# Attention and two MoE layers on one core: the passage to MoE 2 rearranged

## The chip, the cores and the metric

The kernel runs on one core of one Trainium2 chip. Its time is the device time of one execution in microseconds (us); 933.41 us is the median of three runs before the change (931.83 to 934.14). The engines are TensorE (PE; PEld loads its weights), VectorE (DVE), ScalarE (ACT), GpSimd (POOL) and SyncE (SP), each with its own queue of instructions, worked off in order. Transfers are issued from SP, POOL or ACT and run on 16 DMA engines.

## The reference

Three layers follow one another on 2176 tokens of width 512 (4 batches of 32 global and 512 local tokens):

1. Attention: local tokens see the global ones and a window of 32 on either side; global tokens see all.
2. MoE 1: `x = leaky_relu(x @ w_in, 0.01) @ w_out`, with 2048 inner columns.
3. MoE 2, over 8 experts of 512 x 1024 and 1024 x 512. Each token goes to one expert:

```
logits = normalised(x) @ normalised(expert_emb).T / tau
idx    = argmax(logits);  gate = softmax(logits)[idx]
out    = gate * (relu(x @ w1[idx]) @ w2[idx])
```

Inputs and outputs are float32. Products that need it are computed from a high and a low part in the fp32r format, three matmuls for one.

## The kernel before, in words

**Stages.** Attention and MoE 1 run fused, in pairs of token tiles of 128 (17 tiles; the last pair step has three, tiles 14 to 16). A step (i, f) of MoE 1 is `L1` (one slice of 128 inner columns, its leaky ReLU on ScalarE and VectorE) and, a step later, `L2` (its product with `w_out`). Finished tiles are routed: R0 to R3 normalise a tile, transpose it, take its logits, and count its tokens' ranks within their expert; an indirect transfer writes token numbers into a list sorted by expert (`idl`), and the tile's rows go to DRAM (`x2d`).

MoE 2 works on blocks of 128 tokens of one expert, taken from that list. There are up to 24 blocks, in two lanes (even and odd), each lane with its own copy of one expert's weights (`w1a`, `w2a`; `w1b`, `w2b`), loaded by `load_w(s)` only where the plan says that the lane's expert changes. `make_plan(True)` plans the first 6 blocks from tiles 0 to 13 during the last steps of MoE 1; `make_plan(False)`, the late plan, plans the other 18 when the last three tiles are routed.

**The last three tiles.** `Q0` copies a tile from PSUM into x2 and sums its squares; `Q1` transposes it and takes its logits into `lp`; `Q2` finds the expert of all three tiles' tokens, ending with an exponential on ScalarE; `Q3` takes ranks (`rp`) and counts (`cp`) on TensorE; `Q4` turns ranks into list places, issues three indirect scatters into `idl` on POOL and six stores into `x2d` on SP.

**A block.** `block(s)` holds, in this order: `M1(s, 0)` (first half of x @ w1, 12 matmuls, then the ReLU into `hs`); `M2(s-1, 0)`; the split of the next block's first half of w1 (`split_w1`, each split two casts on ScalarE and two subtractions on VectorE, L849 and L850); `HT(s, 0)` (four transposes of hs, evicted to `ht`); `X2(s+1)` (four transposes of the next block's tokens, evicted to `xgT`); `M1(s, 1)`; `M2(s-1, 1)`, which ends in `yo`, scaled on ScalarE and scattered to the output by POOL; `split_w2(s+1, 0)`; `HT(s, 1)`; the two other splits; `load_w(s+3)`. In block 0 `M1(0, 1)` comes ahead. Block s reads its tokens by `gather(s)`, an indirect transfer on POOL from `x2d` by the ids that `load_ids(s)` fetched on SP. At the points "a" to "f" of a block the table `due` puts in routing steps.

**What sets the order.** TensorE is in program order throughout, SP in all blocks, VectorE in blocks 0 to 3 (`manual_schedule`). The other queues are ordered by a scheduler from priorities and estimated readiness; `keep_in_program_order` pins one instruction behind the one traced before it on its engine.

**Buffers.** Tiles with one tag share `bufs` buffers. "half" has 8: the eight halves of MoE 1's weights, then lane b's weights and the split weights of blocks (six buffers). "xs" has 2 and holds `xgT` and tile 16's x2; "x2" has 2 and holds the x2 of tiles 14 and 15 and then `yo`; "x2T" has 2. In PSUM the tags "T", "S", "H" and "Y" have two banks each.

Of the kernel before, what the change touches and what calls it, by code (L numbers as in the profile page):

```python
# [8 lines left out]
F32 = mybir.dt.float32  # L9
# [9 lines left out]
P = 128  # L19
# [5 lines left out]
def kernel(  # L25
# [20 lines left out]
    NT, DM = out.shape  # L46
    DFF = w_in.shape[1]
    E, _, F2 = w1.shape
    HP = H // 2
    NC = SL // P  # L50
    KM = DM // P
    KF = DFF // P
    KF2 = F2 // P
# [360 lines left out]
    rt = {}  # L414
# [121 lines left out]
    NL = 3  # L536
# [19 lines left out]
    def Q1(q):  # L556
        x2 = rt[q, "x2"]
        xp = ps.tile([P, KM, P], F32, tag="T", name="x2p")
        for k in range(KM):
            nc.tensor.transpose(xp[:, k, :], x2[:, k * P:(k + 1) * P], ident)  # L560
        xT = sb.tile([P, KM, P], F32, tag="x2T", bufs=2, name="x2T")
        nc.vector.tensor_copy(xT, xp)
        if q == 0:
            rt["lp"] = ps.tile([P, NL, E], F32, tag="S", name="lp")
        for k in range(KM):
            nc.tensor.matmul(rt["lp"][:, q, :], xT[:, k, :], enT[:, k, :], start=(k == 0), stop=(k == KM - 1))

# [25 lines left out]
    def Q3():  # L593

        ob = lt_["ob3"]
        rp = ps.tile([P, NL, E], F32, tag="T", name="rp")
        nc.tensor.matmul(rp, tri, ob[:, 0:NL], start=True, stop=False)
        nc.tensor.matmul(rp, ones, ob[:, NL].unsqueeze(1).to_broadcast([P, NL, E]), start=False, stop=False)
        for q in range(1, NL):
            nc.tensor.matmul(rp[:, q, :], ones, ob[:, 0, :], start=False, stop=(q == 1 and NL == 2))  # L600
        for q in range(2, NL):
            for o in range(1, q):
                nc.tensor.matmul(rp[:, q, :], ones, ob[:, o, :], start=False, stop=(q == NL - 1 and o == q - 1))
        cp = ps.tile([1, E], F32, tag="T", name="cp")
        for q in range(NL + 1):
            nc.tensor.matmul(cp, ones[:, 0:1], ob[:, q, :], start=(q == 0), stop=(q == NL))
        rt["rp"], rt["cp"] = rp, cp

    def Q4():
        V = nc.vector  # L610
# [115 lines left out]
    def make_plan(early):  # L726
# [21 lines left out]
        if early:  # L748
            mx, ky, k2 = work(1), work(E), work(E)
            V.tensor_reduce(out=mx, in_=nb, axis=AX.X, op=ALU.max)  # L750
            V.scalar_tensor_tensor(out=ky, in0=nb, scalar=mx, in1=rf, op0=ALU.is_equal, op1=ALU.mult)
            V.tensor_reduce(out=mx, in_=ky, axis=AX.X, op=ALU.max)
            V.tensor_scalar(out=ky, in0=ef, scalar1=mx, scalar2=None, op0=ALU.add)
            V.tensor_scalar(out=k2, in0=ky, scalar1=float(E), scalar2=-float(E), op0=ALU.is_ge, op1=ALU.mult)
            V.tensor_tensor(out=ky, in0=ky, in1=k2, op=ALU.add)
            V.tensor_tensor(
                out=lt, in0=ky.unsqueeze(1).to_broadcast([1, E, E]), in1=ky.unsqueeze(2).to_broadcast([1, E, E]),
                op=ALU.is_lt,
            )
        else:  # L760
            V.tensor_tensor(out=nb, in0=nb, in1=taken, op=ALU.subtract)
        V.tensor_tensor(out=pre, in0=lt, in1=nb.unsqueeze(1).to_broadcast([1, E, E]), op=ALU.mult)
        V.tensor_reduce(out=st8, in_=pre, axis=AX.X, op=ALU.add)
        V.tensor_tensor(out=en8, in0=st8, in1=nb, op=ALU.add)
        if early:
            posf = ihf[:, 0:n]
        else:
            pos = work(NLANE, NH)
            tot, h12, hf = work(1), work(NH), work(1)
            V.tensor_reduce(out=tot, in_=nb, axis=AX.X, op=ALU.add)  # L770
            V.tensor_scalar(out=h12, in0=ihf, scalar1=2.0, scalar2=tot, op0=ALU.mult, op1=ALU.is_lt)
            V.tensor_reduce(out=hf, in_=h12, axis=AX.X, op=ALU.add)
            V.tensor_scalar(out=pos[:, 0], in0=ihf, scalar1=hf, scalar2=1000.0, op0=ALU.is_ge, op1=ALU.mult)
            V.tensor_tensor(out=pos[:, 0], in0=pos[:, 0], in1=ihf, op=ALU.add)
            V.tensor_scalar(out=pos[:, 1], in0=ihf, scalar1=hf, scalar2=None, op0=ALU.add)
            V.tensor_copy(plan[:, 0, NBLK:NBLK + 1], tot)
            posf = pos.rearrange("o l i -> o (l i)")
        shp = [1, n, E]
        a1, a2 = work(n, E), work(n, E)
        pb = posf.unsqueeze(2).to_broadcast(shp)  # L780
# [4 lines left out]
        V.tensor_reduce(out=vd, in_=a1, axis=AX.X, op=ALU.add)  # L785
        V.tensor_tensor(out=a2, in0=a1, in1=ef.unsqueeze(1).to_broadcast(shp), op=ALU.mult)
        V.tensor_reduce(out=ex, in_=a2, axis=AX.X, op=ALU.add)
        if early:
            lanewise, at = "o (i l) -> o l i", 0
            V.tensor_reduce(out=taken, in_=a1.rearrange("o n e -> o e n"), axis=AX.X, op=ALU.add)  # L790
            V.tensor_copy(oe, st8)
        else:
            lanewise, at = "o (l i) -> o l i", NE
            V.tensor_tensor(out=oe, in0=st8, in1=taken, op=ALU.subtract)
# [10 lines left out]
        def got(v):  # L805
            return v.rearrange(lanewise, l=NLANE)

        m = n // NLANE
        V.tensor_copy(el[:, :, at + 1:at + 1 + m], got(ex))
        V.tensor_tensor(out=got(ch), in0=got(ex), in1=el[:, :, at:at + m], op=ALU.not_equal)  # L810
# [15 lines left out]
    def load_w(s):  # L826
        if s >= NBLK:
            return
        w1r, w2r = lanes[lane(s)]
        e = nc.sync.value_load(plan[0:1, 1, s:s + 1], min_val=0, max_val=E - 1)  # L830
        cond = nc.sync.value_load(plan[0:1, 2, s:s + 1], min_val=0, max_val=1)
        nc.sync.dma_start(w1r, w1[bass.ds(e, 1)].rearrange("o (k p) f -> p (o k) f", p=P), cond=cond)
        nc.sync.dma_start(w2r, w2[bass.ds(e, 1)].rearrange("o (k p) f -> p (o k) f", p=P), cond=cond)
# [33 lines left out]
    def split_w1(s, j):
        for piece in pieces_w1(s, j):
            piece()

    def split_w2(s, j):
        for piece in pieces_w2(s, j):
            piece()

    def X2(s):
        if s >= NBLK:
# [12 lines left out]
    def M1(s, j):  # L889
        xT = xts[s][0]  # L890
        w = w1s.pop((s, j))
        hp_ = ps.tile([P, DM], F32, tag="H", name="hp2")
        for a, c in ((0, 0), (1, 0), (0, 1)):
            for k in range(KM):
                nc.tensor.matmul(  # L895
                    hp_, xT[:, a, k, :], w[:, c, k, :], start=(a + c + k == 0), stop=(c == 1 and k == KM - 1)
                )
        hs = sb.tile([P, DM], F32, tag="g", bufs=2, name="hs")
        if j == 0:
            nc.scalar.activation(out=hs, in_=hp_, func=AF.Relu)  # L900
        else:
            nc.vector.tensor_scalar(out=hs, in0=hp_, scalar1=0.0, scalar2=None, op0=ALU.max)
        hss[s, j] = hs
# [143 lines left out]
    while k < len(steps):  # L1047
        i, f = steps[k]
        if k == KF * (2 * B - 1) + 6:
            assert not pend_r  # L1050
            plan_constants()
            make_plan(True)
            load_w(0)
            for s in range(NEARLY):
                load_ids(s)
            for s in range(4):
                gather(s)
# [28 lines left out]
            st(t)  # L1086
        if k >= KF * (2 * B - 1) + 10:
            if k == KF * (2 * B - 1) + 10:
                first = pieces_w1(0, 0) + pieces_w1(0, 1) + pieces_w2(0, 0) + pieces_w2(0, 1)
            for piece in first[:2 if len(first) > 6 else 1]:  # L1090
                tc.keep_in_program_order(piece())
            first = first[2 if len(first) > 6 else 1:]
        if slot == LAST and not hold and att is not None:
            att_pool.__exit__(None, None, None)
            att = None
# [4 lines left out]
            )  # L1100
            lanes[0] = lane_a
        k += 1
    lanes[1] = (
        sb.tile([P, KM, F2], F32, tag="half", bufs=8, name="w1b"),
        sb.tile([P, KF2, DM], F32, tag="half", bufs=8, name="w2b"),
    )
    for piece in first:
        piece()
    load_w(1)
    load_w(2)  # L1110
    X2(0)
    L2(*state["prev"])
    for t in range(NL):
        with tc.high_priority(offset=0):
            Q0(t, ys.pop((2 * B - 1, t)))

    def late_plan():
        make_plan(False)
        for q in range(NEARLY, NEARLY + 3):
            load_ids(q)  # L1120

    def block(s, end, begin=0):

# [36 lines left out]
        load_w(s + 3)  # L1160

    due = {
        (0, "a"): [(Q1, (0,)), (Q1, (1,))], (0, "b"): [(Q1, (2,))], (0, "c"): [(Q2, ())],
        (0, "d"): [(Q3, ())], (0, "e"): [(Q4, ())], (1, "a"): [(late_plan, ())],
    }
    NMAN = 4
    NCUT = NBLK - NLANE
# [43 lines left out]
```

## Time and profile before

| | |
|---|---|
| profiled execution | 931.04 us, its span 929.1 us, mean granted clock 0.963 |
| PE busy | 863.6 us, 93% |
| PEld busy | 727.1 us, 78% |
| DVE busy | 639.2 us, 69% |
| ACT busy | 561.6 us, 60% |
| POOL busy | 173.5 us, 19% |
| chain that ended last | PE 73%, DVE 9%, issue 6%, DMA 6%, ACT 5% |

The page cuts the span into 40 slices of 23.2 us and gives the busy share of each in tenths:

```
PE   3766799999999999999999999997899999999997
DVE  6998888444664654554544435556989989999996
PEclk9776799999999999999999999997999999999999
```

Attention alone fills the first five slices, attention with MoE 1 and MoE 1 alone go up to about 621 us, MoE 2 takes the rest. A granted clock of 1.0 is TensorE at 2.4 GHz, 0.5 at 1.2 GHz. In a timeline, equal instructions that follow one another are merged to one row (x12), and the idle time in brackets is that of the engine just ahead of the row, with what ended it. A row of the table by stretches gives the window, its length, the busy us of PE, PEld, DVE, ACT and POOL with their instruction counts, the mean granted clock, the DMA engines' busy share and GB/s.

### The profile page before, as it was taken

What the parts mean: (1) busy time and instruction counts of PE and PEld (TensorE: products, weight loads), DVE (VectorE), ACT (ScalarE), POOL (GpSimd) and SP (SyncE); (2) the same over time, 40 slices, a digit from 0 to 9 for tenths busy, and PEclk for the clock granted to TensorE, in tenths of its full rate; (3) what the DMA queues carried; (4) which work ended last, traced back from release to release, by engine and by line L of the source; (5) the groups of instructions that cost most, each with busy time, mean ns of one, the idle gap of its engine ahead of it and who ended that gap; (6) DMA issues with size and microseconds to landing.
All of it is one profiled execution on the core that took longest, in us unless ns stands there. A gap on an engine that the chain in (4) does not pass through costs nothing.

```text
span 929.1 us, 15882 instructions
## 1 busy us (share of the span) xinstructions
PE 863.6 (93%) x5578; PEld 727.1 (78%) x5578; DVE 639.2 (69%) x1557; ACT 561.6 (60%) x1206; POOL 173.5 (19%) x220
## 2 busy tenths in 40 slices
PE   3766799999999999999999999997899999999997
PEld 2555587888888888888888988986687888888885
DVE  6998888444664654554544435556989989999996
ACT  5877876544544644445433232364687888888885
POOL 3423433000210110010000000120233222231311
PEclk9776799999999999999999999997999999999999
DMA  8875562120122121110000000554315118829550
GB/s 215 197 215 149 146 189 69 33 45 17 29 61 44 25 57 29 44 30 3 13 12 1 24 1 24 193 187 73 24 58 215 35 46 328 276 78 384 191 202 26
DMA packets 104995, 92.68 MB, mean 100 GB/s; under 512 B 73735, under 2 KB 82055, under 8 KB 104914
## 3 DMA queue, kind: packets, MB, share of 16 engines
q1 hardware_dynamic: 97618, 77.47, 27.7%
q0 software_dynamic: 4224, 10.78, 4.2%
q10 hardware_dynamic: 3072, 3.41, 1.2%
q8 instruction: 45, 0.74, 0.4%
q14 instruction: 36, 0.29, 0.1%
HBM read 140.03 MB, written 11.63 MB: 163 GB/s over the span
## 4 chain that ended last, share of the span: by engine, by line
PE 73%; DVE 9%; issue 6%; DMA 6%; ACT 5%; POOL 1%; SPq 1%; POOLq 0%; ACTq 0%; DVEq 0%
PE hps L669 20%; PE hp L895 10%; PE yp L923 9%; PE yp L691 7%; PE yp L693 6%; PE yp L692 6%; PE av L247 3%; PE pp L233 2%; PE sp L199 2%; PE tp L909 2%; DMA qn<-in_q_l_dram 1%; DMA ids<-idl 1%; ACT pr L217 1%; PE lp L499 1%; DVE pr L223 1%
## 5 line engine op out<-in xcount | busy, mean ns | idle before, releaser
L676 ACT COPY gf<-hps 128x256 f32<-128x256 f32 (+1 forms) x144 | 50.2, 360 | 175.2 <-PE hps L669 168.4
L677 DVE SCALAR_TENSOR_TENSOR gf<-gf 128x256 f32<-128x256 f32 (+1 forms) x144 | 60.7, 429 | 129.3 <-ACT gf L676 127.7
L895 PE MATMUL hp<-w1s,xgT 128*128 128x512 f32 x528 | 139.1, 413 | 0.0
L923 PE MATMUL yp<-w2s,ht 128*128 128x512 f32 x528 | 130.9, 396 | 1.0 <-DVEq L1175 1.0
L923 PEld LDWEIGHTS yp<-w2s,ht 128*128 128x128 f32 x528 | 98.8, 188 | 25.7 <-DVEq L1175 1.4
L895 PEld LDWEIGHTS hp<-w1s,xgT 128*128 128x128 f32 x528 | 100.0, 196 | 21.4
L691 PE MATMUL yp<-woh,g 128*128 128x512 f32 x272 | 114.8, 422 | 0.0
L693 PE MATMUL yp<-woh,g 128*128 128x512 f32 x272 | 107.7, 396 | 0.0
L692 PE MATMUL yp<-wol,g 128*128 128x512 f32 x272 | 107.7, 396 | 0.0
L680 DVE TENSOR_TENSOR g<-gf,g 128x256 fp32r<-128x256 f32 (+1 forms) x144 | 57.7, 409 | 39.3 <-ACT g L679 35.0
L669 PE MATMUL hps<-xs,wih 128*128 128x256 f32 x448 | 75.7, 291 | 5.7 <-ACT gf L676 4.2
L679 ACT CAST g<-gf 128x256 fp32r<-128x256 f32 (+1 forms) x144 | 55.3, 395 | 36.1 <-DVE gf L677 36.1
L669 PEld LDWEIGHTS hps<-xs,wih 128*128 128x128 f32 x448 | 65.0, 189 | 12.5 <-ACT gf L676 4.9
L669 PE MATMUL hps<-xs,wil 128*128 128x256 f32 x448 | 71.3, 281 | 0.0
L669 PE MATMUL hps<-xl,wih 128*128 128x256 f32 x448 | 71.2, 280 | 0.0
L217 ACT ACTIVATE pr<-pr,nm 128x224 f32<-128x224 f32 x128 | 60.6, 475 | 2.7 <-DVE nm L211 1.8
L693 PEld LDWEIGHTS yp<-woh,g 128*128 128x128 f32 x272 | 51.2, 188 | 12.7 <-DVE g L680 0.2
L669 PEld LDWEIGHTS hps<-xs,wil 128*128 128x128 f32 x448 | 60.9, 189 | 0.0
L669 PEld LDWEIGHTS hps<-xl,wih 128*128 128x128 f32 x448 | 60.9, 189 | 0.0
L691 PEld LDWEIGHTS yp<-woh,g 128*128 128x128 f32 x272 | 51.3, 189 | 11.7 <-issue 4.5
L850 DVE TENSOR_TENSOR w2s<-w2a,w2s 128x1024 fp32r<-128x1024 f32 x48 | 56.7, 1218 | 2.8 <-ACT w2s L849 2.6
L850 DVE TENSOR_TENSOR w1s<-w1a,w1s 128x1024 fp32r<-128x1024 f32 x48 | 56.5, 1217 | 1.8 <-ACT w1s L849 1.7
(257 smaller groups left out, 1705.1 us busy)
## 6 DMA issues: line engine op xcount, KB each, us to landing
w1a<-in_moe_w_dram SPq DMA_DIRECT2D x12, 2048.0 KB
w2a<-in_moe_w_dram SPq DMA_DIRECT2D x12, 2048.0 KB
w1b<-in_moe_w_dram SPq DMA_DIRECT2D x12, 2048.0 KB
w2b<-in_moe_w_dram SPq DMA_DIRECT2D x12, 2048.0 KB
raw<-in_moe_w_in_dram SPq DMA_DIRECT2D x13, 512.0 KB
raw<-in_moe_w_out_dram SPq DMA_DIRECT2D x13, 512.0 KB
x2d<-x SPq DMA_DIRECT2D x16, 256.5 KB
kn<-in_k_l_dram SPq DMA_DIRECT2D x31, 128.0 KB
```

The lines of the kernel that those rows point to most:

```text
L217: nc.scalar.activation(out=pr, in_=pr, func=AF.Exp, bias=nm[:, j:j + 1], scale=-1.0, accum_out=sm[:, j:j + 1],)
L669: nc.tensor.matmul(hps, ws[a][:, k], xs[c][k], start=(a + c + k == 0), stop=((a, c) == (1, 0) and k == KM - 1))
L676: nc.scalar.copy(gf, hps[:, cs])
L677: nc.vector.scalar_tensor_tensor(out=gf, in0=gf, scalar=0.01, in1=gf, op0=ALU.mult, op1=ALU.max)
L679: nc.scalar.copy(g[:, 0], gf)
L680: nc.vector.tensor_tensor(out=g[:, 1], in0=gf, in1=g[:, 0].bitcast(F32), op=ALU.subtract)
L691: nc.tensor.matmul(yp, g[:, 0], hi, start=(f == 0), stop=False)
L692: nc.tensor.matmul(yp, g[:, 0], lo, start=False, stop=False)
L693: nc.tensor.matmul(yp, g[:, 1], hi, start=False, stop=(f == KF - 1))
L850: nc.vector.tensor_tensor(out=w[:, 1, c], in0=src[:, c], in1=w[:, 0, c].bitcast(F32), op=ALU.subtract)
L895: nc.tensor.matmul(hp_, xT[:, a, k, :], w[:, c, k, :], start=(a + c + k == 0), stop=(c == 1 and k == KM - 1))
L923: nc.tensor.matmul(yp, ht[:, a, f, :], w[:, c, f, :], start=(j + a + c + f == 0), stop=(j == c == 1 and f == 3))
```

## The change

- The buffers of lane b (`w1b`, `w2b`) are taken, and its load issued, in step 10 of the last pair of MoE 1, ahead of the first block's split weights; those are then w1 alone, one piece a step. The split of block 0's w2 comes after `Q0`, pinned.
- `Q1` stops at the transposed tile; the logits become a step of their own, `Q1L`. Logits, ranks and counts share one PSUM tile `lr` with tag "Y", in place of `lp` ("S"), `rp` and `cp` ("T").
- `make_plan` becomes a generator of five pieces. `due` places `Q1L`, `Q2`, `Q3`, `Q4` and the pieces later: `Q2` from point "c" to "e" of block 0, `Q3` and `Q4` to "a" and "c" of block 1, the pieces to block 1 "e", "f" and block 2 "a", "d", "e".
- The ScalarE casts of splits for block 1 are pinned behind what stands ahead of them in the code.
- The second ReLU of blocks 0 to 4 moves from VectorE to ScalarE.

```diff
@@ -560,8 +560,13 @@
             nc.tensor.transpose(xp[:, k, :], x2[:, k * P:(k + 1) * P], ident)
         xT = sb.tile([P, KM, P], F32, tag="x2T", bufs=2, name="x2T")
         nc.vector.tensor_copy(xT, xp)
+        rt[q, "xT"] = xT
+
+    def Q1L(q):
         if q == 0:
-            rt["lp"] = ps.tile([P, NL, E], F32, tag="S", name="lp")
+            rt["bank"] = ps.tile([P, 2 * NL + 1, E], F32, tag="Y", name="lr")
+            rt["lp"] = rt["bank"][:, 0:NL]
+        xT = rt.pop((q, "xT"))
         for k in range(KM):
             nc.tensor.matmul(rt["lp"][:, q, :], xT[:, k, :], enT[:, k, :], start=(k == 0), stop=(k == KM - 1))
 
@@ -593,7 +598,7 @@
     def Q3():
 
         ob = lt_["ob3"]
-        rp = ps.tile([P, NL, E], F32, tag="T", name="rp")
+        rp = rt["bank"][:, NL:2 * NL]
         nc.tensor.matmul(rp, tri, ob[:, 0:NL], start=True, stop=False)
         nc.tensor.matmul(rp, ones, ob[:, NL].unsqueeze(1).to_broadcast([P, NL, E]), start=False, stop=False)
         for q in range(1, NL):
@@ -601,10 +606,11 @@
         for q in range(2, NL):
             for o in range(1, q):
                 nc.tensor.matmul(rp[:, q, :], ones, ob[:, o, :], start=False, stop=(q == NL - 1 and o == q - 1))
-        cp = ps.tile([1, E], F32, tag="T", name="cp")
+        cp = rt["bank"][0:1, 2 * NL, :]
         for q in range(NL + 1):
             nc.tensor.matmul(cp, ones[:, 0:1], ob[:, q, :], start=(q == 0), stop=(q == NL))
         rt["rp"], rt["cp"] = rp, cp
+        rt.pop("bank")
 
     def Q4():
         V = nc.vector
@@ -759,6 +765,7 @@
             )
         else:
             V.tensor_tensor(out=nb, in0=nb, in1=taken, op=ALU.subtract)
+        yield
         V.tensor_tensor(out=pre, in0=lt, in1=nb.unsqueeze(1).to_broadcast([1, E, E]), op=ALU.mult)
         V.tensor_reduce(out=st8, in_=pre, axis=AX.X, op=ALU.add)
         V.tensor_tensor(out=en8, in0=st8, in1=nb, op=ALU.add)
@@ -775,6 +782,7 @@
             V.tensor_scalar(out=pos[:, 1], in0=ihf, scalar1=hf, scalar2=None, op0=ALU.add)
             V.tensor_copy(plan[:, 0, NBLK:NBLK + 1], tot)
             posf = pos.rearrange("o l i -> o (l i)")
+        yield
         shp = [1, n, E]
         a1, a2 = work(n, E), work(n, E)
         pb = posf.unsqueeze(2).to_broadcast(shp)
@@ -785,6 +793,7 @@
         V.tensor_reduce(out=vd, in_=a1, axis=AX.X, op=ALU.add)
         V.tensor_tensor(out=a2, in0=a1, in1=ef.unsqueeze(1).to_broadcast(shp), op=ALU.mult)
         V.tensor_reduce(out=ex, in_=a2, axis=AX.X, op=ALU.add)
+        yield
         if early:
             lanewise, at = "o (i l) -> o l i", 0
             V.tensor_reduce(out=taken, in_=a1.rearrange("o n e -> o e n"), axis=AX.X, op=ALU.add)
@@ -805,6 +814,7 @@
         def got(v):
             return v.rearrange(lanewise, l=NLANE)
 
+        yield
         m = n // NLANE
         V.tensor_copy(el[:, :, at + 1:at + 1 + m], got(ex))
         V.tensor_tensor(out=got(ch), in0=got(ex), in1=el[:, :, at:at + m], op=ALU.not_equal)
@@ -866,11 +876,11 @@
 
     def split_w1(s, j):
         for piece in pieces_w1(s, j):
-            piece()
+            (tc.keep_in_program_order if s < 2 else id)(piece())
 
     def split_w2(s, j):
         for piece in pieces_w2(s, j):
-            piece()
+            (tc.keep_in_program_order if s < 2 else id)(piece())
 
     def X2(s):
         if s >= NBLK:
@@ -896,7 +906,7 @@
                     hp_, xT[:, a, k, :], w[:, c, k, :], start=(a + c + k == 0), stop=(c == 1 and k == KM - 1)
                 )
         hs = sb.tile([P, DM], F32, tag="g", bufs=2, name="hs")
-        if j == 0:
+        if j == 0 or s < 5:
             nc.scalar.activation(out=hs, in_=hp_, func=AF.Relu)
         else:
             nc.vector.tensor_scalar(out=hs, in0=hp_, scalar1=0.0, scalar2=None, op0=ALU.max)
@@ -1049,7 +1059,8 @@
         if k == KF * (2 * B - 1) + 6:
             assert not pend_r
             plan_constants()
-            make_plan(True)
+            for _ in make_plan(True):
+                pass
             load_w(0)
             for s in range(NEARLY):
                 load_ids(s)
@@ -1086,10 +1097,15 @@
             st(t)
         if k >= KF * (2 * B - 1) + 10:
             if k == KF * (2 * B - 1) + 10:
-                first = pieces_w1(0, 0) + pieces_w1(0, 1) + pieces_w2(0, 0) + pieces_w2(0, 1)
-            for piece in first[:2 if len(first) > 6 else 1]:
+                lanes[1] = (
+                    sb.tile([P, KM, F2], F32, tag="half", bufs=8, name="w1b"),
+                    sb.tile([P, KF2, DM], F32, tag="half", bufs=8, name="w2b"),
+                )
+                load_w(1)
+                first = pieces_w1(0, 0) + pieces_w1(0, 1)
+            for piece in first[:1]:
                 tc.keep_in_program_order(piece())
-            first = first[2 if len(first) > 6 else 1:]
+            first = first[1:]
         if slot == LAST and not hold and att is not None:
             att_pool.__exit__(None, None, None)
             att = None
@@ -1100,24 +1116,21 @@
             )
             lanes[0] = lane_a
         k += 1
-    lanes[1] = (
-        sb.tile([P, KM, F2], F32, tag="half", bufs=8, name="w1b"),
-        sb.tile([P, KF2, DM], F32, tag="half", bufs=8, name="w2b"),
-    )
-    for piece in first:
-        piece()
-    load_w(1)
     load_w(2)
     X2(0)
     L2(*state["prev"])
     for t in range(NL):
         with tc.high_priority(offset=0):
             Q0(t, ys.pop((2 * B - 1, t)))
+    for piece in pieces_w2(0, 0) + pieces_w2(0, 1):
+        tc.keep_in_program_order(piece())
+
+    plan_pieces = make_plan(False)
 
     def late_plan():
-        make_plan(False)
-        for q in range(NEARLY, NEARLY + 3):
-            load_ids(q)
+        if next(plan_pieces, "done") == "done":
+            for q in range(NEARLY, NEARLY + 3):
+                load_ids(q)
 
     def block(s, end, begin=0):
 
@@ -1160,8 +1173,9 @@
         load_w(s + 3)
 
     due = {
-        (0, "a"): [(Q1, (0,)), (Q1, (1,))], (0, "b"): [(Q1, (2,))], (0, "c"): [(Q2, ())],
-        (0, "d"): [(Q3, ())], (0, "e"): [(Q4, ())], (1, "a"): [(late_plan, ())],
+        (0, "a"): [(Q1, (0,)), (Q1, (1,))], (0, "b"): [(Q1L, (0,)), (Q1L, (1,)), (Q1, (2,))], (0, "d"): [(Q1L, (2,))],
+        (0, "e"): [(Q2, ())], (1, "a"): [(Q3, ())], (1, "c"): [(Q4, ())], (1, "e"): [(late_plan, ())],
+        (1, "f"): [(late_plan, ())], (2, "a"): [(late_plan, ())], (2, "d"): [(late_plan, ())], (2, "e"): [(late_plan, ())],
     }
     NMAN = 4
     NCUT = NBLK - NLANE
```

## Rows read from the trace of the kernel before

**Rows 1.** Table by stretches of 20 us

```profile
620.00:640.00 20.00, 16.11 (x81) 13.11 (x80) 6.72 (x18) 13.45 (x22) 2.27 (x2) 0.83 0.49 188
640.00:660.00 20.00, 15.31 (x64) 12.17 (x63) 19.17 (x55) 9.90 (x13) 3.07 (x3) 0.83 0.62 46
```

**Rows 2.** Waits of 620 to 720 us (total us, times, longest us)

```profile
PE tp L909 <- DVE hs L902: 5.8, 2, 3.8
...
PE cp L606 <- DVE xgT L884: 3.3, 1, 3.3
...
PE lp L566 <- DVE x2T L562: 2.7, 3, 0.9
```

**Rows 3.** Timeline of PE (start, duration, what; in brackets idle before, releaser)

```profile
621.62 2.96 PE L895 MATMUL hp<-w1s,xgT 128*128 128x512 f32 x12
...
625.87 1.06 PE L566 MATMUL lp<-enT,x2T 128*128 128x8 f32 x8 [0.85 <-DVE x2T L562]
...
630.00 5.09 PE L895 MATMUL hp<-w1s,xgT 128*128 128x512 f32 x12
...
643.66 5.07 PE L895 MATMUL hp<-w1s,xgT 128*128 128x512 f32 x12
...
662.63 4.21 PE L895 MATMUL hp<-w1s,xgT 128*128 128x512 f32 x12
...
703.84 3.08 PE L895 MATMUL hp<-w1s,xgT 128*128 128x512 f32 x12
...
728.54 0.60 PE L909 MATMUL tp<-ident,hs 128*128 128x128 f32 x4
...
741.06 0.60 PE L909 MATMUL tp<-ident,hs 128*128 128x128 f32 x4
```

**Rows 4.** Timeline of DVE, same columns

```profile
636.33 0.22 DVE L580 TENSOR_SCALAR sl<-sl,tau_sb 128x3 f32<-128x3 f32 x1
...
639.12 2.35 DVE L850 TENSOR_TENSOR w1s<-w1b,w1s 128x1024 fp32r<-128x1024 f32 x2
641.39 0.68 DVE L912 TENSOR_TENSOR ht<-tp,ht 128x512 fp32r<-128x512 f32 x1
...
642.58 0.17 DVE L612 TENSOR_TENSOR sr<-rp,base_e 128x24 f32<-128x24 f32 x1
...
643.91 2.34 DVE L850 TENSOR_TENSOR w2s<-w2b,w2s 128x1024 fp32r<-128x1024 f32 x2
...
651.31 0.15 DVE L741 TENSOR_SCALAR wk<-cp 1x8 f32<-1x8 f32 x1
...
652.32 0.21 DVE L762 TENSOR_TENSOR wk<-wk 1x64 f32<-1x64 f32 x1
...
655.74 0.14 DVE L794 TENSOR_TENSOR wk<-wk 1x8 f32<-1x8 f32 x1
...
657.67 2.34 DVE L850 TENSOR_TENSOR w1s<-w1a,w1s 128x1024 fp32r<-128x1024 f32 x2
```

**Rows 5.** Timeline of ACT, same columns

```profile
623.75 0.20 ACT L553 ACTIVATION_READ_ACCUMULATOR sq<-x 128x1 f32 x1
...
630.55 1.99 ACT L849 CAST w2s<-w2b 128x1024 fp32r<-128x1024 f32 x2 [3.46 <-DMA w2b<-in_moe_w_dram]
...
654.87 0.59 ACT L883 CAST xgT<-xgp 128x512 fp32r<-128x512 f32 x1 [0.81 <-DMA x2d<-x]
```

**Rows 6.** Timeline of SP's DMA issues, same columns

```profile
587.34 8.17 SPq L824 DMA_DIRECT2D ids<-idl  x6
...
643.94 2.72 SPq L627 DMA_DIRECT2D x2d<-x  x6
...
670.40 2.56 SPq L824 DMA_DIRECT2D ids<-idl  x3
```

**Rows 7.** Groups by line, 620 to 704 us (count | busy us, mean ns | idle)

```profile
L902 DVE TENSOR_SCALAR hs<-hp 128x512 f32<-128x512 f32 x5 | 3.4, 681 | 6.9 <-PE hp L895 6.9
...
L900 ACT ACTIVATE hs<-hp 128x512 f32<-128x512 f32 x5 | 3.0, 599 | 8.8 <-PE hp L895 8.8
```

## The prediction

> **What bounds the kernel now.** I read the 40 slices of the page first. TensorE is at nine tenths or more nearly everywhere from the sixth slice on; the exception is slices 28 and 29, and its clock dips in the first of them. Next, the table by stretches shows that dip as 620 to 660 us: in the two 20 us stretches PE is busy 16.11 and 15.31 us at a mean granted clock of 0.83, and VectorE goes from 6.72 us of work in the first to 19.17 in the second [rows 1]. So this is the passage from MoE 1 to MoE 2, in which VectorE first has nothing and then too much. Third, the waits of 620 to 720 us name what PE stood idle for: 5.8 us for the ReLU hs on VectorE (L902), in two pauses of 3.8 and 2.0; 3.3 us for xgT before the counts (L606); 2.7 us for the transposed tile x2T before the logits (L566) [rows 2]. That is 11.8 us. Last, the timeline of PE shows what the pauses do to the clock: a group of 12 block matmuls takes 2.96 us, but 5.09, 5.07 and 4.21 after them [rows 3]. The excess is 2.13 + 2.11 + 1.25 = 5.5 us at the lower level (1.2 GHz, a granted clock of 0.5).
>
> From the first matmul of block 0 (621.62) to that of block 5 (703.84) it takes 82.2 us [rows 3]. A steady block takes 741.06 - 728.54 = 12.52 us; with 2.80 for each of its four groups M1 and M2 and 0.44 for each of its three transposes (HT twice, X2) that sum comes out. Block 0 has no M2 and costs 6.9, four more blocks 50.1, the last tiles' transposes and logits 3 x 0.44 + 3 x 1.06 = 4.5, ranks 0.6: 62.1 us. Hence about 20 us is the most that any rearrangement can return.
>
> **The change, part by part.** I follow VectorE's queue, because it keeps its order of the code in blocks 0 to 3 and is the busy one. Its prices, as steps from start to start: a whole split (two L850) 641.39 - 639.12 = 2.27; a small eviction (ht, xgT, x2T) 0.60; Q2 639.12 - 636.33 = 2.79; Q4 643.91 - 642.58 = 1.33; the late plan 657.67 - 651.31 = 6.36, of which its first piece 1.01, the second and third 3.42, the last two 1.93 [rows 4].
>
> *Second lane loaded in MoE 1.* In the trace the casts of block 1's w2 wait 3.46 us for w2b's arrival [rows 5]. Now the lane's two loads come behind the six id loads, which end at 595.5 [rows 6], with half a dozen MoE 1 steps still to go; w1b and w2b are there long before block 0. SP loses nothing: the skipped loads behind them wait for splits as before. Worth by itself about nothing on PE, but the splits of block 1 may start at once. Its price: block 0's w2 gives up its buffers and is split after Q0. Q0 ends on ScalarE at 623.95 [rows 5]; four casts of about 1.0 follow, and four subtractions of 1.17 on VectorE from 625.0 to 629.7. Before, they lay beside full PE work.
>
> *Logits apart from the transposes.* PE: M1(0,0), eight transposes without a wait, M1(0,1) to 628.1 at full clock. The copies of x2T queue behind the w2 subtractions: 630.3 and 630.9, so PE waits 2.2 us there (0 if the copies come first, which the order of the code doesn't say for work ahead of block 0). Q1L(0) and Q1L(1), 1.06 each [rows 3], to 632.5; Q1(2), copy at 633.6.
>
> *Q2, Q3, Q4 later; ranks and counts in one bank.* The 3.3 us wait of the counts goes: they no longer need a bank that xgT of block 1 must empty. VectorE from 633.6: split w1 of block 1 to 635.9, ht and xgT to 637.1, Q2 to 639.9. What is late next: the cast of w2(1,0) is now pinned behind the exponential, so the next split's first half begins at 641.1, not 639.9. Then split 643.4, ht 644.0, two splits 648.5, Q4 649.9. On PE M1(1,0) runs from 637.1, ranks when Q2 is done, M1(1,1) from 646.3 to 649.1. Q4's six stores, three scatters and, behind the plan, three id loads move too. The id loads stood at 670.40, 26.5 us after Q4's end (643.91) [rows 4, 6]; 649.9 + 26.5 = 676.4, and block 6's gather behind them has until block 5 is under way (after 690). This cover of 14 us or more hides it. The yo of block 0 needs a buffer that one of the moved stores reads; ScalarE may wait up to 2 us there, and I charge 1.0.
>
> *Plan in five pieces, ReLUs on ScalarE.* VectorE in block 1: split 652.1, ht and xgT 653.3. M1(2,0) starts there; before it was 662.63 [rows 3], so 9.3 us are won. Then piece one 654.3, split, ht, two splits 661.7, pieces two and three 665.2, split 667.4, ht and xgT 668.6: M1(3,0) starts at 668.6, after an idle 2.7 on PE. Pieces four and five 670.6, split, ht and split 675.7, so M1(3,1) waits 0.6. From there PE is the later one: M1(4,0) 681.9, and with no VectorE ReLU in front (the second pause of rows 2, 2.0 us, is block 4's) M1(5,0) at 694.5 against 703.84 [rows 3]. That is 9.3 us. The ReLUs cost ScalarE 0.60 each for 0.68 on VectorE [rows 7], and ScalarE has 6 to 10 us of every 20 free here [rows 1]: nothing.
>
> ScalarE: Activation LUTs (the Trainium skill, Rules for kernel authors) says to use VectorE, not ScalarE, for relu, up to about 3 times faster there in bf16. In this float32 case the rows say 0.60 against 0.68; three times 0.68 would be 2 us on ScalarE, which its idle time would still nearly cover. The measurement decides.
>
> *Clock.* The idle 2.7 before M1(3,0) likely costs as the 3.8 before M1(2,0) did (1.25), at least half of it seen: 0.9. A slow M1(1,0) is covered by VectorE's queue, which ends last there. Sum: 9.3 - 1.0 - 0.9 = 7.4 us. The ends: 12 with the copies ahead of the w2 subtractions and no late yo; 4 with two more pauses and cold starts.
>
> **Rivals.** *(A) A store takes the wait's place.* The buffers of tag xs are two: one holds block 1's xgT, the other the last tile's x2 until Q4's stores have read it. In the trace the cast of xgT for block 2 is released by that store at 654.87 [rows 5], 11.0 us after Q4's end (643.91) [rows 4], hidden by the plan. If it takes that buffer again, it waits until 649.9 + 11.0 = 660.9, VectorE behind it, and M1(2,0) starts at 662.1 instead of 653.3, with the whole plan still ahead: M1(5,0) at 703, a gain of 0.8 us less a cold start: 933. For it: nothing in the order forbids it. Against: M1(1,1) ends at 649.1 and frees the other buffer sooner, and a buffer is given to who can have it first. A gentler form: the stores land quickly after the last issue (2.72 us for six [rows 6]); M1(2,0) then starts near 656, and 5 us are won (928.5).
>
> DMA: Bandwidth & Descriptors (the Trainium skill, Anatomy of one DMA) puts the fixed cost of a transfer at about 2 us, mostly the receipt of the write; by it this gentler form would hold. The trace does not agree: its cast was released 8.2 us after the last of the six issues.
>
> *(B) Slower: (A) with Q4 late.* Q2, the pinned casts and Q4 now stand in one line. With the store's buffer taken, each us that Q4 ends after 649.9 is a us on M1(2,0); parity is passed at about 650.8, and at 654 (the logits at the lower clock, and the casts behind exp late by a split) the loss is 3.2: 936.6. For it: rows 3 show how readily the clock falls among the logits. Against: it needs both.
>
> *(C) Copies first.* VectorE takes x2T before the w2 subtractions; the 2.2 us pause never comes: gain 11 to 12, 922.
>
> **How the numbers follow.** The profiled execution took 931.04 us (span 929.1 and 1.9 around it); the median of the three runs shown is 933.41, 2.4 above it. A forecast of 931.04 - 7.4 = 923.6 for such a run is 926.0 for the median. About 0.3% (2.8 us) is what a measurement of this kernel can tell from no change. Chances: main line 0.52 (922 to 930 by itself), C 0.10, gentle A 0.05, A 0.21 (933, counted as no change mostly), B 0.12. Faster by over 0.3%: 0.52 + 0.10 + 0.05 and none of A: 0.66 with a little taken off for a main line that comes out small; within: 0.22; slower: 0.12. The range reaches to A on one side, which is 7 us above the forecast, and a little past C on the other: 920.5 to 934.
>
> **What would show it.** Right: in the profile after, no PE wait on hs (L902) before block 5 and none of the counts on xgT; the first M1 of block 2 near 653 and that of block 5 near 694 to 696; steady blocks of 12.52 us behind it; VectorE without idle time from 633 to 680; the PE wait before the first logits near 2. Wrong: an xgT cast in block 2 released by the x2d store near 661 (A), later than 664 (B), or PE waiting at block 6 for its gather.

## The result, and the profile after

The changed kernel takes 921.17 us (919.5 to 922.43) against 932.82 us before: a ratio of 0.9876, 95% interval [0.9857, 0.9895]. Run once more beside the last experiments it was 920.35 against 932.09, 0.9872 [0.9857, 0.9887]. The forecast was 926.0, range 920.5 to 934.0, faster with a chance of 0.66. The sign and the range were right; 7.4 us were forecast and 11.7 came. The range was met in its lowest part: the main line had 922 to 930 us for itself, and the stretch down to 920.5 had been added for rival C.

The profiled execution took 921.0 us, its span is 919.3. The table by stretches answers to [rows 1] (window, length, busy us of PE, PEld, DVE, ACT, POOL with counts, granted clock, DMA share, GB/s):

```profile
620.00:640.00 20.00, 17.89 (x98) 14.78 (x96) 12.50 (x25) 13.68 (x24) 1.92 (x2) 0.92 0.05 14
640.00:660.00 20.00, 18.45 (x97) 14.80 (x96) 19.72 (x31) 18.73 (x24) 3.77 (x2) 1.00 0.13 40
680.00:700.00 20.00, 19.96 (x97) 16.15 (x96) 20.00 (x21) 16.61 (x23) 18.82 (x4) 1.00 0.27 90
```

PE's clock is down only in the first stretch (0.92, before 0.83 in both), and VectorE is busy 12.50 us there, before 6.72: the empty time ahead of the passage has been filled. The waits of PE from 620 to 720 us, against [rows 2]:

```profile
PE hp L905 <- DVE xgT L894: 3.9, 2, 2.1
PE tp L919 <- ACT hs L910: 3.4, 2, 1.9
```

11.8 us have become 7.4 (2.11 + 1.79 + 1.55 + 1.90): none on a ReLU on VectorE, none on the counts, none on x2T. In their place are two on the low part of xgT and two on a ReLU on ScalarE. The timeline of PE, against [rows 3]:

```profile
622.46 2.96 PE L905 MATMUL hp<-w1s,xgT 128*128 128x512 f32 x12
...
626.05 3.05 PE L905 MATMUL hp<-w1s,xgT 128*128 128x512 f32 x12
628.94 1.85 PE L571 MATMUL lr<-enT,x2T 128*128 128x8 f32 x16
...
636.66 3.68 PE L905 MATMUL hp<-w1s,xgT 128*128 128x512 f32 x8 [2.11 <-DVE xgT L894]
...
645.17 0.66 PE L919 MATMUL tp<-ident,hs 128*128 128x128 f32 x4 [1.55 <-ACT hs L910]
...
652.06 3.04 PE L905 MATMUL hp<-w1s,xgT 128*128 128x512 f32 x12
...
664.57 1.18 PE L905 MATMUL hp<-w1s,xgT 128*128 128x512 f32 x4
667.53 2.13 PE L905 MATMUL hp<-w1s,xgT 128*128 128x512 f32 x8 [1.79 <-DVE xgT L894]
...
691.93 3.08 PE L905 MATMUL hp<-w1s,xgT 128*128 128x512 f32 x12
...
712.22 0.66 PE L919 MATMUL tp<-ident,hs 128*128 128x128 f32 x4 [1.90 <-ACT hs L910]
```

M1(0,1) takes 3.05 us where it took 5.09, and the logits behind it (628.94) follow without a pause. Behind the pause of 2.11 the clock is down (eight matmuls take 3.68 us); the same eight at 667.53, behind 1.79 us, take 2.13. M1(2,0) starts 29.6 us after M1(0,0), before 41.0. From M1(0,0) to M1(5,0) it is 691.93 - 622.46 = 69.5 us, before 82.2; I call this stretch *the passage* below. So 12.75 us are won there. 1.9 are lost again at 712.22, in block 6, and block 0 itself starts 0.84 us later (622.46 against 621.62): 12.75 - 1.90 - 0.84 = 10.0, which is the difference of the two profiled executions (931.04 - 921.0). VectorE, against [rows 4]:

```profile
625.97 1.29 DVE L562 COPY x2T<-x2p 128x512 f32<-128x512 f32 x2 [4.10 <-PE x2p L560]
627.17 3.49 DVE L860 TENSOR_TENSOR w2s<-w2a,w2s 128x1024 fp32r<-128x1024 f32 x3
631.31 0.69 DVE L562 COPY x2T<-x2p 128x512 f32<-128x512 f32 x1 [0.65 <-PE x2p L560]
...
633.05 2.35 DVE L860 TENSOR_TENSOR w1s<-w1b,w1s 128x1024 fp32r<-128x1024 f32 x2
...
636.52 0.22 DVE L585 TENSOR_SCALAR sl<-sl,tau_sb 128x3 f32<-128x3 f32 x1
...
639.91 2.36 DVE L860 TENSOR_TENSOR w2s<-w2b,w2s 128x1024 fp32r<-128x1024 f32 x2 [1.23 <-ACT w2s L859]
...
647.33 0.18 DVE L618 TENSOR_TENSOR sr<-lr,base_e 128x24 f32<-128x24 f32 x1
...
651.52 0.68 DVE L894 TENSOR_TENSOR xgT<-xgp,xgT 128x512 fp32r<-128x512 f32 x1
...
666.81 0.67 DVE L894 TENSOR_TENSOR xgT<-xgp,xgT 128x512 fp32r<-128x512 f32 x1
```

The first two copies of x2T stand *ahead* of the w2 subtractions (625.97, then 627.17). Behind Q2 VectorE waits 1.23 us for the pinned cast, and from there on it has no pause until 707. Q2 itself takes 639.91 - 1.23 - 636.52 = 2.16 us. The 2.79 that the prediction read from the kernel before held a wait for the logits:

```profile
637.56 0.18 DVE L582 TENSOR_TENSOR lg<-lp,sl 128x24 f32<-128x24 f32 x1 [0.80 <-PE lp L566]
```

ScalarE, against [rows 5]; the issues behind it answer to [rows 6]:

```profile
625.46 0.60 ACT L910 ACTIVATE hs<-hp 128x512 f32<-128x512 f32 x1 [0.67 <-PE hp L905]
625.96 3.88 ACT L859 CAST w2s<-w2a 128x1024 fp32r<-128x1024 f32 x4
...
638.72 0.22 ACT L596 ACTIVATE lg<-lg 128x24 f32<-128x24 f32 x1 [4.49 <-DVE lg L595]
638.85 1.98 ACT L859 CAST w2s<-w2b 128x1024 fp32r<-128x1024 f32 x2
...
644.52 0.59 ACT L910 ACTIVATE hs<-hp 128x512 f32<-128x512 f32 x1
...
649.28 0.58 ACT L893 CAST xgT<-xgp 128x512 fp32r<-128x512 f32 x1
...
708.61 0.69 ACT L940 ACTIVATE yo<-yp,gate 128x512 f32<-128x512 f32 x1 [5.09 <-DMA out_dram<-yo,ids]
```

The issues on SP, same columns (SPq is its DMA queue):

```profile
598.19 0.38 SPq L842 DMA_DIRECT2D w1b<-in_moe_w_dram  x1
...
648.65 2.74 SPq L633 DMA_DIRECT2D x2d<-x  x6
...
676.68 2.95 SPq L834 DMA_DIRECT2D ids<-idl  x3
```

On ScalarE the ReLU of M1(0,0) stands ahead of the four casts of block 0's w2, so the first of them starts at 625.96 and VectorE's first w2 subtraction at 627.17. The exponential (L596) waits 4.49 us for VectorE, and six pinned casts stand between it and hs of block 1 (644.52). The cast of xgT for block 2 (649.28) starts without a wait, within a microsecond of the first store's issue: it did not get the buffer that the stores read. The id loads stand at 676.68. The one wait of ScalarE that PE pays for is at 708.61, for the scatter of an earlier yo.

### The profile page after: what moved, and what is told of

Same layout as the page of the kernel before. It is cut to its first block, busy times and chain, and to the rows that moved or that the text cites. A ratio compares the mean times of both kernels' runs of the same rounds, so it can differ in the third digit from the quotient of the medians.

```text
span 919.3 us, 15875 instructions
## 1 busy us (share of the span) xinstructions
PE 855.3 (93%) x5578; PEld 719.7 (78%) x5578; DVE 634.9 (69%) x1552; ACT 562.4 (61%) x1211; POOL 191.1 (21%) x220
## 4 chain that ended last, share of the span: by engine, by line
PE 69%; DMA 7%; issue 7%; DVE 7%; ACT 6%; POOL 3%; SPq 1%; POOLq 0%; ACTq 0%; DVEq 0%
PE hps L675 20%; PE hp L905 8%; PE yp L697 7%; PE yp L933 7%; PE yp L699 6%; PE yp L698 6%; DMA out_dram<-yo,ids 3%; PE av L247 2%; PE pp L233 2%; POOL xg L849 2%; PE sp L199 2%; ACT pr L217 2%; DMA ids<-idl 1%; PE lp L499 1%; PE tp L919 1%
## 5 line engine op out<-in xcount | busy, mean ns | idle before, releaser
L905 PE MATMUL hp<-w1s,xgT 128*128 128x512 f32 x528 | 136.1, 405 | 3.9 <-DVE xgT L894 3.9
L905 PEld LDWEIGHTS hp<-w1s,xgT 128*128 128x128 f32 x528 | 96.7, 190 | 25.3 <-DVE xgT L894 5.3
L685 ACT CAST g<-gf 128x256 fp32r<-128x256 f32 (+1 forms) x144 | 55.4, 395 | 36.7 <-DVE gf L683 36.7
L675 PE MATMUL hps<-xs,wil 128*128 128x256 f32 x448 | 71.3, 281 | 0.0
L849 POOL DMA_INDIRECT xg<-x2d,ids x24 | 49.6, 2068 | 58.3 <-PE hps L675 21.8
L941 POOL DMA_INDIRECT out_dram<-yo,ids x22 | 31.7, 1441 | 141.0 <-ACT yo L940 127.1
```

Of the source, the lines that this page charges most:

```text
L675: nc.tensor.matmul(hps, ws[a][:, k], xs[c][k], start=(a + c + k == 0), stop=((a, c) == (1, 0) and k == KM - 1))
L685: nc.scalar.copy(g[:, 0], gf)
L849: nc.gpsimd.indirect_dma_start(out=xg, out_offset=None, in_=x2d[:, :], in_offset=bass.IndirectOffsetOnAxis(ap=ids[:, s:s + 1].bitcast(U32) ...
L905: nc.tensor.matmul(hp_, xT[:, a, k, :], w[:, c, k, :], start=(a + c + k == 0), stop=(c == 1 and k == KM - 1))
```

## The experiments

Each was timed in five rounds beside the kernel before, which the ratios are to. The passage is read from each one's trace; it repeats well (69.47 and 69.51 us in the two profiles of the changed kernel), while block 0 starts anywhere from 619.5 to 624.5 us, though no experiment changes more of MoE 1 than the last six steps. The medians hold that scatter, the passage does not. A longer passage is not all lost, either: where it takes 75 us or more, the pause in block 6 does not come. A dash in the last column: no such wait.

| kernel | us | ratio, 95% interval | passage | PE wait in block 6 |
|---|---|---|---|---|
| before | 932 to 933 | 1 | 82.2 | - |
| changed | 921.17 | 0.9876 [0.9857, 0.9895] | 69.5 | 1.9 |
| e1_relu_back | 930.1 | 0.9961 [0.9942, 0.9980] | 79.4 | - |
| e2_plan_whole | 932.05 | 0.9994 [0.9981, 1.0007] | 81.6 | - |
| e2b_plan_whole_ids_late | 923.36 | 0.9910 [0.9891, 0.9929] | 75.3 | - |
| e3_copies_pinned | 926.75 | 0.9927 [0.9905, 0.9948] | 75.8 | - |
| e4_load_late | 920.77 | 0.9863 [0.9845, 0.9882] | 68.9 | 1.7 |
| e5_routing_early | 926.79 | 0.9936 [0.9917, 0.9956] | 78.4 | - |
| e6_banks_apart | 921.51 | 0.9890 [0.9867, 0.9912] | 70.7 | 1.7 |
| e10_no_pins | 920.13 | 0.9879 [0.9857, 0.9902] | 71.3 | 1.9 |
| e9_relu_alone | 925.57 | 0.9938 [0.9922, 0.9955] | 76.2 | - |
| e7_yo4 | 919.45 | 0.9867 [0.9853, 0.9881] | 69.5 | - |
| e8_late_yo4 | 917.93 | 0.9846 [0.9833, 0.9859] | 70.2 | - |

The theory was that VectorE's one in-order queue between 633 and 668 us sets the passage, so that what counts is what stands in it and where. The rival was that the weights' feed and the shared bank made the gain.

**e1_relu_back.** Edit:

```diff
-        if j == 0 or s < 5:
+        if j == 0:
```

> The changed kernel with the second ReLU of blocks 0 to 4 back on VectorE. Queue theory (what stands in VectorE's queue between 633 and 668 us sets the passage): 0.6 us more per block in that queue, and HT(1,1), HT(2,1), HT(3,1) wait on hs for about 1, 4 and 2 us, so M1(5,0) comes 4 to 6 us later: 926 us. Feed theory (the gain is the early load of lane b and the shared bank; the ReLU only changes sides): within 1 us of the changed kernel's 921.2.

It lost more than the queue theory said, 9.9 us of passage. Its PE waits from 618 to 725 us:

```profile
PE tp L919 <- DVE hs L912: 6.7, 2, 4.4
PE lr L571 <- DVE x2T L562: 1.7, 1, 1.7
```

The pauses on hs have the priced size: 4.4 before HT(2,1) and 2.3 before HT(4,1) (priced for HT(3,1)), and 1.1 before HT(1,1), which the view puts down to the plan. The price lacked two things: the 1.7 us for an x2T copy, which now stands behind the first hs and three subtractions, and the clock, as M1(3,0) took 4.76 us after the longest pause. The feed theory, which had no loss here, falls.

**e2_plan_whole, e2b_plan_whole_ids_late.** Edits:

```diff
-(1, "c"): [(Q4, ())], (1, "e"): [(late_plan, ())], ...
+(1, "c"): [(Q4, ())] + [(late_plan, ())] * 5,    # both; in e2 the ids load here
+(2, "e"): [(late_ids, ())],     # e2b alone: the three id loads, as late as in the changed kernel
```

In e2b `late_plan` itself no longer loads the ids.

> The changed kernel with the five pieces of the late plan run at one point, right behind Q4 in block 1. Queue theory: 5.4 us more ahead of xgT for block 2, so M1(2,0) starts near 658 instead of 652, after a pause of about 6 us and at the lower clock; the later pieces are gone, so M1(3,0) loses only 3 to 4 of it: 925 to 926 us. Rival (VectorE's sum is the same, so the place does not count): 921 to 922.

> As e2_plan_whole, the plan in one piece behind Q4, but the three id loads stay where the pieces had them, at point e of block 2. If VectorE's queue alone made up the loss of e2: 932 again. If the half of it was SP, where the id loads stood ahead of the load of block 4 and held ScalarE's cast for 8.2 us: the pause of 5 us before HT(3,1) goes, block 2 still starts late, 925 to 927.

The first lost everything, twice what I had priced. Its ScalarE shows the wait:

```profile
683.57 1.99 ACT L859 CAST w1s<-w1a 128x1024 fp32r<-128x1024 f32 x2 [8.18 <-DMA w1a<-in_moe_w_dram]
```

Its SP shows what stood ahead:

```profile
679.30 2.57 SPq L834 DMA_DIRECT2D ids<-idl  x3
683.42 0.09 SPq L842 DMA_DIRECT2D w1a<-in_moe_w_dram  x1
```

The id loads wait for the scatters until 679.30; behind them on SP stands the load of block 4 (which the plan skips: its issue takes 0.09 us, one that runs 0.38; but it must be passed), and the cast waits 8.18 us for it. With the id loads at their later point the passage is 75.3 (and the time 923.36, less than expected), so of the 12.2 us that e2 lost in the passage, 6.3 were SP's and 5.9 VectorE's, each with what the clock added. In the changed kernel, cutting the plan up therefore does two things: it spreads VectorE's work, and it lets block 4's load go ahead of the id loads.

**e3_copies_pinned.** Edit, which puts the copies behind the w2 subtractions:

```diff
-        nc.vector.tensor_copy(xT, xp)
+        tc.keep_in_program_order(nc.vector.tensor_copy(xT, xp))
```

> The changed kernel with the copies of x2T put behind the four w2 subtractions on VectorE, as the main line of the forecast had it. If that line priced the pause rightly: PE waits about 2 us before the first logits, VectorE's later queue shifts by about 1.9 us, 923 us. Rival (slack further on takes it): 921 to 921.5, with the pause in the trace all the same.

Its PE:

```profile
634.37 3.58 PE L571 MATMUL lr<-enT,x2T 128*128 128x8 f32 x16 [3.21 <-DVE x2T L562]
...
651.66 1.12 PE L919 MATMUL tp<-ident,hs 128*128 128x128 f32 x4 [3.08 <-ACT hs L910]
...
653.28 4.97 PE L905 MATMUL hp<-w1s,xgT 128*128 128x512 f32 x12
```

The pause before the logits is 3.21 us; the 16 matmuls behind it take 3.58 us (1.85 in the changed kernel). A second pause of 3.08 before HT(1,0) leaves M1(1,1) at 4.97 us. The passage is 6.3 us longer than the changed kernel's, and 926.75 is neither the 923 expected nor the rival's 921. The prediction's main line, with its charges for the yo and the clock, puts the passage at 72.9 + 1.9 = 74.8 us; this kernel, which has that line's order, took 75.8. That the two are so close is partly luck. M1(2,0) starts 36.7 us after M1(0,0), where the line had 31.7: the logits ran at the lower level, and HT(1,0) waited on ScalarE's casts. Against that, PE waits 0.94 us in M1(3,0) where the line had 2.7, and no clock is lost behind it.

**e4_load_late.** Edit (w1b and w2b are allocated and loaded behind the loop again, and the pinned w2 pieces behind Q0 go back ahead of it):

```diff
-                lanes[1] = (...)
-                load_w(1)
-                first = pieces_w1(0, 0) + pieces_w1(0, 1)
+                first = pieces_w1(0, 0) + pieces_w1(0, 1) + pieces_w2(0, 0) + pieces_w2(0, 1)
...
+    lanes[1] = (...)
+    for piece in first:
+        piece()
+    load_w(1)
...
-    for piece in pieces_w2(0, 0) + pieces_w2(0, 1):
-        tc.keep_in_program_order(piece())
```

> The changed kernel with the placement of before for lane b's load and for the split of block 0's w2 (that split again within MoE 1, the load behind it). Queue theory: 4.6 us of subtractions leave VectorE's queue ahead of 633 us, of which about 1 us can be had, as the third x2T copy waits for PE until 631: 920 us. Feed theory: the casts of block 1 wait for w1b and w2b as before, 2 to 4 us lost: 923 to 925.

0.6 us shorter in the passage, and equal in time within the intervals: the early load of lane b, with the later split of block 0's w2 that it needs, wins nothing.

**e5_routing_early.** Edit:

```diff
-(0, "a"): [(Q1, (0,)), (Q1, (1,))], (0, "b"): [(Q1L, (0,)), (Q1L, (1,)), (Q1, (2,))], (0, "d"): [(Q1L, (2,))],
-(0, "e"): [(Q2, ())], (1, "a"): [(Q3, ())], (1, "c"): [(Q4, ())], (1, "e"): [(late_plan, ())],
+(0, "a"): [(Q1, (0,)), (Q1L, (0,)), (Q1, (1,)), (Q1L, (1,))], (0, "b"): [(Q1, (2,)), (Q1L, (2,))],
+(0, "c"): [(Q2, ())], (0, "d"): [(Q3, ())], (0, "e"): [(Q4, ())], (1, "e"): [(late_plan, ())],
```

> The changed kernel with logits, Q2, Q3 and Q4 at their points of before (one bank, the plan in pieces and the ReLUs as changed). Queue theory: VectorE's sum up to M1(3,0) stays, but PE waits three times for x2T (0.9 us each) and starts M1(0,1) or M1(1,0) at the lower clock: 2 to 3 us lost, 923 to 924. Rival (the later places are worth nothing once the plan is cut up): 921.

8.9 us of passage lost, 5.6 in time, where 2 to 3 were expected. The waits for x2T come back (2.5 us), M1(0,1) takes 5.16 us again, and the low clock runs on into M1(1,0). But the places are not alone in it. Its PE and ScalarE:

```profile
638.93 0.24 PE L611 MATMUL lr<-ob,ones 128*1 128x8 bf16 x4
...
634.87 0.60 ACT L910 ACTIVATE hs<-hp 128x512 f32<-128x512 f32 x1 [6.22 <-PE hp L905]
...
638.95 1.98 ACT L859 CAST w1s<-w1b 128x1024 fp32r<-128x1024 f32 x2
...
655.97 0.59 ACT L893 CAST xgT<-xgp 128x512 fp32r<-128x512 f32 x1 [2.92 <-DMA x2d<-x]
```

With Q2 this early, the pins put all casts for block 1 behind its exponential: the first starts at 638.95 (630.22 in the changed kernel), though ScalarE had stood idle for 6.22 us. So 8.9 us is what the early places cost together with the pins; the early places without the pins were not run. The counts (L611) follow without a wait: with the shared bank they need no later place. And the cast of xgT for block 2 does wait for the stores here, as rival A of the prediction had it: it is released 11.2 us after Q4's end (644.81), which costs VectorE 1.42 us and PE nothing.

**e6_banks_apart.** Edit:

```diff
-            rt["bank"] = ps.tile([P, 2 * NL + 1, E], F32, tag="Y", name="lr")
-            rt["lp"] = rt["bank"][:, 0:NL]
+            rt["lp"] = ps.tile([P, NL, E], F32, tag="S", name="lp")
...
-        rp = rt["bank"][:, NL:2 * NL]
+        rp = ps.tile([P, NL, E], F32, tag="T", name="rp")
...
-        cp = rt["bank"][0:1, 2 * NL, :]
+        cp = ps.tile([1, E], F32, tag="T", name="cp")
```

> The changed kernel with logits, ranks and counts in three PSUM tiles with the tags of before. With ranks this late, the counts find their bank free; but both T banks are then held until Q4 and the plan's first piece have read them, so X2(2) waits about 2 us for Q4. Queue theory: that pause lies ahead of one that VectorE sets anyway, 0 to 1 us lost, 921 to 922. Feed theory (the shared bank is the gain): the 3.3 us of before come back, 924 to 925.

As the queue theory had it. Its new waits:

```profile
PE tp L917 <- DVE ht L920: 2.9, 1, 2.9
...
PE xgp L889 <- DVE sr L616: 1.6, 1, 1.6
```

X2(2) waits 1.6 us for Q4 to free a bank, and HT(0,1) 2.9 us until the subtraction to ht(0,0) has left the one S bank that lp leaves free; the passage is 1.2 us longer. The 3.3 us of before do not come back, so the later place removes them without the shared bank. As e5 has the bank without the place and no such wait either, each of the two is enough.

**e10_no_pins.** Edit, in `split_w1` and `split_w2`:

```diff
-            (tc.keep_in_program_order if s < 2 else id)(piece())
+            piece()
```

> The changed kernel without the pins on the casts of block 1's splits; ScalarE then has six of these eight casts ahead of hs(0,1), and all ahead of ht(0,0) and xgT(1). The forecast charged the pins 1.2 us, so without them 920. Rival (order on ScalarE counts as that on VectorE does): ht, xgT and hs come 3 to 6 us later than now, HT(0,1) and M1(1,0) wait, 924 to 927.

The time, 920.13, is the first forecast's number, but it cannot be told from the changed kernel's; the passage goes the rival's way and is 1.8 us longer. PE waits 2.9 us for hs(0,1) and 2.2 for xgT, behind the casts. The 1.2 us that VectorE waits behind Q2 do go with the pins, and 3.0 us for ht ahead of Q2 (635.42) come in their place.

**e9_relu_alone.** Edit, in the kernel before and alone:

```diff
-        if j == 0:
+        if j == 0 or s < 5:
```

> The kernel before with only the second ReLU of blocks 0 to 4 on ScalarE. If the edits add up, it takes away what e1_relu_back lost, some 9 us: 924. If the parts need one another (queue theory): HT(1,1) no longer waits behind the plan, but M1(2,0) then waits for xgT behind the same plan, so 1 to 1.5 us of the 3.8 come back, and block 4's 2.0: 930.

Between the two, at 925.57: the passage is 6.0 us shorter, not 3 and not 9. Its PE:

```profile
658.89 1.18 PE L895 MATMUL hp<-w1s,xgT 128*128 128x512 f32 x4
661.82 2.13 PE L895 MATMUL hp<-w1s,xgT 128*128 128x512 f32 x8 [1.75 <-DVE xgT L884]
```

M1(2,0) does wait for xgT behind the plan, but only 1.75 us: it had begun with the four matmuls that need the high part alone, and behind the pause the other eight run at the full clock (2.13 us). All the other edits without the ReLU are worth 82.2 - 79.4 = 2.8; with it 76.2 - 69.5 = 6.7. The parts need one another, as the queue theory says, but less than I had priced.

**e7_yo4, e8_late_yo4.** Edit (e8 also has the edit of e4):

```diff
-        yo = sb.tile([P, DM], F32, tag="x2", bufs=2, name="yo")
+        yo = sb.tile([P, DM], F32, tag=("x2", "x2T")[s % 2], bufs=2, name="yo")
```

> The changed kernel with yo's tiles taken in turn from the two buffers of x2 and the two of x2T, which are free from block 1 on. In the changed kernel ScalarE waits 5.1 us at 708.6 for the scatter of an earlier yo to leave its buffer, and PE 1.9 us at 712 for the ReLU behind it. If that is the whole of it: that pause goes, 919.3 us. Rival (the late scatters on POOL hold the gathers too, and the wait reappears there): 921.

> e4_load_late (lane b loaded and block 0's w2 split where they were before) with the four buffers for yo: the passage of e4, 68.9 us, without its pause of 1.7 us in block 6: 918.5 to 919.

ScalarE of e7:

```profile
703.85 0.69 ACT L940 ACTIVATE yo<-yp,gate 128x512 f32<-128x512 f32 x1 [0.84 <-issue]
```

The yo that waited at 708.61 no longer waits for a scatter, and PE's pause in block 6 is gone: from M1(5,0) to M1(7,0) it is 25.0 us, in the changed kernel 27.2. The medians (919.45 beside 920.35) do not tell the two apart. e8 is the fastest version, 917.93 us; each of its runs (at most 918.80) is below each of the changed kernel's beside it (at least 919.44). Its passage, 70.2, is not the 68.9 expected: behind a pause of 2.44 us in M1(3,0) eight matmuls took 3.44 us, in e4, behind 2.42, they took 2.13. It is not shorter than e7's; why its median is 1.5 us lower stays open, and the intervals of the two touch.

> The changed kernel itself, beside the three others on the same chip: 921 to 922 us.

It took 920.35 us, a little less than that, with the same passage of 69.5.

## Why the prediction was right in sign and range, and 4 us off

- *"The copies of x2T queue behind the w2 subtractions: 630.3 and 630.9, so PE waits 2.2 us there"*. This step failed. The line had the casts of w2 start right behind Q0; ScalarE did the ReLU of M1(0,0) first, so the first subtraction started at 627.17 only, and the copies, which could start at 625.97, went ahead. PE had no pause: the forecast's rival C, which stood at 922 and had a chance of 0.10. That the range holds 921.17 is owed to C. e3 built the order of the main line and took 926.75; its passage agrees with that line's sum, but not part by part.
- *The chain through VectorE's queue.* Forecast from M1(0,0): 31.7 us to M1(2,0), 60.3 to M1(4,0), 72.9 to M1(5,0). Measured: 29.6, 56.7, 69.5. Of the 3.4 us that it came out ahead, 2.0 are VectorE's: it starts on block 1's split 10.6 us after M1(0,0), not 12.0 (the copies' order), and Q2 takes 2.16 us, not 2.79, which held a wait of 0.80. The rest lies behind M1(3,0): there the four matmuls on the high part of xgT are done before the pause, so eight follow it and not twelve (0.8 us), and the wait of 0.6 before M1(3,1) does not come. The line also had VectorE end last all through block 1; at HT(1,0) it was ScalarE's queue (1.55 us).
- *"The idle 2.7 before M1(3,0) likely costs as the 3.8 before M1(2,0) did": 0.9 charged.* The pause was 1.79 and the granted clock stayed at 1.0 from 640 us on: nothing.
- *"ScalarE may wait up to 2 us there, and I charge 1.0"* for yo. The cost is 1.9 us, but in block 6 and not in block 0: not the stores held the buffer, but a scatter on POOL behind three slow gathers. That the two charges add up to the same 1.9 us is chance.
- *The wait of the counts* went, as said: the bank is reason enough (e5), and so is the later place (e6). *The early load* is worth nothing on PE, as said (e4). *The cast pinned behind the exponential* delays VectorE by 1.23 us, forecast 1.2.
- *"That is 9.3 us" with the ReLUs "nothing" on ScalarE.* ScalarE did carry them. e1 shows that 9.9 us of passage hang on them once the rest is in place.
- *Rival A* did not come: xgT of block 2 got the other buffer. In e5 the wait for the store came 11.2 us after Q4 (worked out: 11.0), but hurt little there, since block 2 started late for other reasons (657.52); what it would cost in the changed kernel's order was not tried. *B* needed A. The section of the Trainium skill cited there is headed for transfers issued from GpSimd, and these stores are issued from SP, so the 8.2 us are no test of it.

## What to carry to other kernels

Follow the queue that ends last, and ask of every item in it what stands behind it on the other engines: here five ReLUs of 0.6 us, behind splits and a 6 us plan, were worth 6 to 10 us of the passage, since a pause of TensorE can be paid a second time in its clock. Where a scheduler is free to choose between two orders, price both and look which one is ready first: the copies here were ready as soon as the transposes were, the subtractions only a cast later. A skipped transfer still has its place in its queue, and what it stands behind counts.

## What the runs showed of the hardware that was not expected

Indirect gathers on POOL, which take 1.0 to 1.9 us to issue elsewhere in the passage and just behind it, took up to 7.7 us where VectorE had not one pause (20.00 us busy of 20, 680 to 700 us):

```profile
661.66 1.05 POOL L849 DMA_INDIRECT xg<-x2d,ids  x1 [0.30 <-PE hp L905]
...
683.79 7.07 POOL L849 DMA_INDIRECT xg<-x2d,ids  x1 [0.31 <-issue]
691.16 7.69 POOL L849 DMA_INDIRECT xg<-x2d,ids  x1 [0.30 <-issue]
...
689.90 0.67 DVE L922 TENSOR_TENSOR ht<-tp,ht 128x512 fp32r<-128x512 f32 x1
...
697.91 0.67 DVE L922 TENSOR_TENSOR ht<-tp,ht 128x512 fp32r<-128x512 f32 x1
```

Both end a usual issue's time after VectorE has left three whole splits (L860) that follow one another without a gap: 690.86 is 0.96 us after the eviction that starts at 689.90, and 698.85 is 0.94 us after that of 697.91. The 7.11 us issue in e3 and the 5.99 in e9 end 0.95 us after such an eviction, too. In the kernel before, with VectorE busy 19.05 of 20 in the same stretch, a gather beside two splits took 1.67 us: it ended at 685.44, 1.01 us after the one split gave way to the next (684.43). So a long issue goes with an unbroken run of splits, but splits do not always lengthen it; that they are its cause was not tested.

The Trainium skill (SBUF — State Buffer, section SBUF: two separate sides) describes an exclusive lock on a port pair that VectorE and GpSimd share; a VectorE instruction with two inputs in SBUF takes it only against a GpSimd instruction that reads SBUF. The subtractions of the splits have two such inputs, and the times above fit; that a gather's issue counts as such an instruction, no run here shows.

The clock does not follow the length of the pause alone. Behind 2.11 us the eight matmuls of M1(1,0) took 3.68 us in the changed kernel (granted clock 0.92 from 620 to 640 us); e7 has the same pause at the same place, and they took 2.13 (1.00):

```profile
636.15 2.13 PE L905 MATMUL hp<-w1s,xgT 128*128 128x512 f32 x8 [2.11 <-DVE xgT L894]
```

The passage is 69.5 us in both. *"A slow M1(1,0) is covered by VectorE's queue"* is right as to the cover, but it is ScalarE's queue that ends last: HT(1,0) waits for hs, which stands behind the exponential and six pinned casts, and starts 22.7 us after M1(0,0) in both kernels (645.17 - 622.46 and 644.66 - 621.96).
